# Weight splits on GpSimd instead of VectorE, and the low part of p ahead of the evacuations

## The chip, the cores and the metric

The kernel runs on one core of one Trainium2 chip. A core has a matrix engine (TensorE, "PE" in the profile, with its weight loads as "PEld"), a vector engine (VectorE, "DVE"), a scalar engine (ScalarE, "ACT"), a general engine (GpSimd, "POOL") and a queue engine (SyncE, "SP") that issues all DMA transfers of this kernel. Each engine takes its instructions strictly in the order in which the program lists them; engines wait for one another with semaphores. The metric is the device time of one execution in microseconds (us). The kernel before takes 931.03 us, the median of three runs from 930.53 to 931.16.

## The reference

```python
x  = A_x                                  # 1 x 2048 x 640, float32
xn = layernorm(x)
s  = attention(xn, wqkv, wo)              # 32 heads of 20, causal, window of 256 keys
h  = relu(xn @ w1 + b1) ** 2              # 640 -> 1536
g  = silu(h @ w2 + b2)                    # 1536 -> 640
return x + s * g
```

Here `attention` makes q, k and v with `xn @ wqkv`, takes a softmax over the keys that are at most 255 places behind a query, sums the values and multiplies with `wo`.

## The kernel before, in words

All products are made in pieces that together carry nearly float32 accuracy. A float32 operand is split into a high part (rounded to the matrix engine's float32 form) and a low part (the operand minus its high part); a product is then three matmuls, high by high, high by low and low by high. Splitting a weight therefore takes one ScalarE instruction that writes the high part and one subtraction that writes the low part. q, k and v are stored as three bfloat16 parts each and packed so that one matmul with 120 rows makes the scores of a head.

The program has three stretches. First (up to about 120 us) x is normalized and transposed, v is made for all rows, and q and k of the first group of heads. The weights of this stretch are split by `split_w` (line 177), whose subtraction is on GpSimd already. Then comes the main loop (lines 958 to 1009): 16 pairs of heads by 16 blocks of 128 rows give 256 steps and a dozen steps of run-out. A step works on five blocks of different age at once: the scores of block s (`scores`, L432) with their row maxima (`maxima`, L444, on VectorE); for the block of nine steps ago the transposed scores (`scores_t`, L476) and their exponentials p (`exps`, L483, on ScalarE) with the causal mask (L484 and L486, on GpSimd); for the block of ten steps ago the high half of p (`high`, L491, ScalarE); for that of eleven steps ago the low half (`low`, L497, VectorE, p minus its high half, called pl); and every second step the sums over the values (L511). The attention results are joined by three GpSimd instructions (L524, L525, L528) once in four steps and stored with a DMA (`o<-on`).

Attention alone does not fill TensorE, so each step also takes a portion of other matmuls from a generator, `filler`. Its stages, in order, are: q and k of the later groups of heads (`qkps`, L562), then for each half of the hidden layer and each quarter of the rows the first layer (`hps`, L562) and the second (`yps`, L824), and after the loop the output product (`wops`). `fill(amount)` hands out a fixed estimated time per step, so the order of the matmuls is fixed when the program is written, not while it runs. The results of a filler group leave PSUM in `evac` functions that are put on a list (`pending`, `late`) and emitted by `flush()` in the middle of the next step: for `qkps` a ScalarE copy and a VectorE subtraction (L730), later a GpSimd subtraction (L734, slo); for `hps` a ScalarE relu and square, a VectorE product (L782, sq) and a GpSimd subtraction (L783, hl); for `yps` a VectorE addition (L828).

The weights of the filler's stages are brought in pieces. `piece_pair` queues a piece that has its high and low part in one tile each (the q and k weights of a group and wo), `piece_lin` one whose parts lie in a row of tiles (w1 and w2, where a part can cross from one tile into the next and is then subtracted in two instructions). `issue` starts the DMA of a piece into one of three raw buffers; two steps later at the earliest `tick()` emits its split, at most one piece per step, in the middle of the step, ahead of the step's exponentials. In the loop there are two such pieces for each of three groups of heads, five for each half of w1, six for each half of w2 and five for wo: 33 pieces, 37 subtractions.

The middle of a step reads before the change:

```python
flush()
if d:
    low(*d)
tick()
if b:
    exs[b] = (exps(*b, *stp), stp[1])
```

Of the kernel before, what the change touches and what calls it, by code (L numbers as in the profile page):

```python
# [46 lines left out]
def f32(ap):  # L47
    return ap.bitcast(F32)
# [3 lines left out]
def attn_mlp_kernel(ctx: ExitStack, tc, x, wqkv, wo, w1, b1, w2, b2, out):  # L52
    nc = tc.nc
# [440 lines left out]
    def low(p, kb):  # L494
        ph, p32, n = phs.pop((p, kb))
        pl = at4.tile([P, 2, 3 * P], F16, tag="pl", bufs=PB - 1, name="pl")
        nc.vector.tensor_sub(pl[:, :, :n], p32[:, :, :n], ph[:, :, :n])  # L497
        pts[p, kb] = (ph, pl)
# [52 lines left out]
    def flush(upto=None):  # L551
        for f in late[:]:
            f()
        late.clear()
        while pending and (upto is None or flushed[0] < upto):
            flushed[0] += 1
            pending.pop(0)()
# [7 lines left out]
    def lin(tiles, off, n):  # L565
        done = 0
        while done < n:
            t, o = divmod(off + done, KC * BT)
            m = min(n - done, KC * BT - o)
            yield tiles[t][:, o:o + m], done, m  # L570
            done += m

    def lin1(tiles, off, n):
        t, o = divmod(off, KC * BT)
        return tiles[t][:, o:o + n]
# [5 lines left out]
    def issue(amount):  # L581
        credit[0] = min(credit[0] + amount, amount)
        while credit[0] > 0 and start_pieces(1):
            credit[0] -= 1.0
        while bulk and credit[0] > 0:
            cost, fn = bulk.pop(0)
            fn()
            credit[0] -= cost
# [27 lines left out]
    def release(n, force=False):  # L616
        done = []
        while started and len(done) < n:
            tag, at_, go = started[0]
            if not force and (tag in shut or state[2] < at_ + AGE):  # L620
                break
            done.append(started.pop(0)[2])
        return done

    def tick():
        for f in release(1):
            f()
            held[0] -= 1
# [9 lines left out]
    def piece(tag, src, go):  # L638
        def start():
            n = src.shape[-1]  # L640
            raw = wgt.tile([P, FHALF], F32, tag="wraw", bufs=RAW, name="raw")[:, :RAWN[tag[0]]]
            if len(src.shape) == 3:
                raw = raw.rearrange("p (c n) -> p c n", n=n)
            nc.sync.dma_start(raw, src)
            return lambda: go(raw)
        queue.append((tag, start))
# [3 lines left out]
    def piece_lin(tag, tiles, ohi, olo, src):  # L650
        n = src.shape[-1]

        def go(raw):
            t_ = tiles()
            for ap, o, m in lin(t_, ohi, n):
                nc.scalar.activation(ap, raw[:, o:o + m], AF.Copy)
            cuts = sorted({o for o in range(0, n + 1, P) if (ohi + o) % (KC * BT) == 0 or (olo + o) % (KC * BT) == 0} | {0, n})
            for c0, c1 in zip(cuts, cuts[1:]):
                nc.vector.tensor_sub(lin1(t_, olo + c0, c1 - c0), raw[:, c0:c1], f32(lin1(t_, ohi + c0, c1 - c0)))  # L659
        piece(tag, src, go)  # L660

    def piece_pair(tag, hi, lo, src):
        def go(raw):
            nc.scalar.activation(hi(), raw, AF.Copy)
            nc.vector.tensor_sub(lo(), raw, f32(hi()))
        piece(tag, src, go)

    def lazy(make):
# [282 lines left out]
    with tc.manual_schedule(engines={E_.PE, E_.Activation, E_.DVE, E_.Pool, E_.SP}):  # L951
# [6 lines left out]
        for s in range(steps):  # L958
# [32 lines left out]
                stp = scores_t(*b)  # L991
            post_all()
            issue(RATE)
            flush()
            if d:
                low(*d)
            tick()
            if b:
                exs[b] = (exps(*b, *stp), stp[1])
# [41 lines left out]
```

## Time and profile before

| | |
|---|---|
| time, median of 3 runs | 931.03 us (930.53 to 931.16) |
| the profiled execution: its time, its span | 931.16 us, 929.5 us |
| TensorE busy | 903.4 us, 97% |
| VectorE busy | 754.9 us, 81% |
| ScalarE busy | 670.0 us, 72% |
| GpSimd busy | 529.2 us, 57% |
| subtractions of weight pieces in the loop | 26 at L659, 11 at L665 |
| granted TensorE clock | 1.0 throughout |

The span runs from the first to the last instruction; 1.66 us of the execution lie outside it. An engine counts as busy while one of its instructions runs, also where that instruction has started and is held up; matmuls overlap, so a busy TensorE is not a TensorE at its peak, and waiting shows better in the time that a step takes than in the share. The chain of waits follows the end of the program back through what released each instruction. The tables by stretch give, for windows of the span, each engine's busy time and in brackets its number of instructions; asked for one line of the kernel, they give that line's alone. Since a step has two score matmuls at L432, their number tells the number of steps in a window.

### The profile page before, as it was taken

The numbers are of one execution on the slowest core, as the hardware profiler recorded it, in microseconds if no ns is written. First come the engines' busy times: TensorE is split into PE (matmuls) and PEld (weight loads), VectorE is DVE, ScalarE is ACT, GpSimd is POOL, SyncE is SP. The second block draws the span as 40 slices with busy tenths as digits, with TensorE's granted clock in tenths as the row PEclk, the third lists the DMA queues.
The fourth block names the chain that finished last, engine by engine and source line by source line (L and its number), as shares of the span: only waits on it lengthen the run. The fifth ranks groups of instructions, "written<-read, shape, count | busy, mean of one in ns | idle before, by whom it ended". The sixth has DMA issues, their size and how long they took to land.

```text
span 929.5 us, 21774 instructions
## 1 busy us (share of the span) xinstructions
PE 903.4 (97%) x7632; PEld 728.6 (78%) x7632; DVE 754.9 (81%) x2031; ACT 670.0 (72%) x1282; POOL 529.2 (57%) x832
## 2 busy tenths in 40 slices
PE   8999999999998899999999999999999999999998
PEld 7899976676665578788688778678688687789998
DVE  7695478989989988988888989987988988875554
ACT  5354338888988986987886987977987977984221
POOL 6010017887877884785774865885764965871000
PEclk9999999999999999999999999999999999999999
DMA  6998686677777454244254153365174264055873
GB/s 229 310 398 299 200 262 202 220 226 232 233 238 250 125 186 128 87 164 133 56 195 160 58 149 118 105 221 147 55 252 136 73 212 141 24 188 170 285 279 114
DMA packets 130803, 168.79 MB, mean 182 GB/s; under 512 B 44100, under 2 KB 91268, under 8 KB 128132
## 3 DMA queue, kind: packets, MB, share of 16 engines
q1 hardware_dynamic: 130692, 167.39, 55.1%
q8 instruction: 60, 0.98, 0.4%
q14 instruction: 51, 0.42, 0.1%
HBM read 96.15 MB, written 70.91 MB: 180 GB/s over the span
## 4 chain that ended last, share of the span: by engine, by line
PE 75%; DVE 12%; ACT 4%; DMA 3%; issue 3%; POOL 2%; SPq 1%; DVEq 0%; POOLq 0%; ACTq 0%
PE yps L824 15%; PE hps L562 13%; PE qkps L562 8%; PE wops L562 8%; PE sps L432 7%; PE ops L511 7%; PE stps L476 7%; PE vps L243 6%; DVE junk L444 3%; DVE pl L497 2%; DVE w L659 2%; PE qkps L201 1%; ACT p L483 1%; DVE st L142 1%; DMA xt<-in_A_x_dram 1%
## 5 line engine op out<-in xcount | busy, mean ns | idle before, releaser
L483 ACT ACTIVATE p<-stps,ebias 128x384 f32<-128x384 f32 (+2 forms) x512 | 258.4, 557 | 82.7 <-PE stps L476 69.9
L444 DVE CUSTOM_DVE_ANT_0 junk<-sps,mask 128x384 bf16<-128x384 f32 (+2 forms) x512 | 251.2, 527 | 62.7 <-PE sps L432 55.5
L497 DVE TENSOR_TENSOR pl<-p,ph 128x768 f16<-128x768 f32 (+2 forms) x256 | 241.0, 941 | 2.6 <-ACT ph L491 2.2
L484 POOL TENSOR_SCALAR_AFFINE_SELECT p<-p 128x256 f32<-128x256 f32 x256 | 145.9, 570 | 137.0 <-ACT p L483 127.6
L491 ACT ACTIVATE ph<-p 128x768 f16<-128x768 f32 (+2 forms) x256 | 206.0, 805 | 15.0 <-POOL p L486 13.2
L562 PE MATMUL hps<-xb,w 128*128 128x512 f32 x630 | 198.2, 430 | 0.0
L824 PE MATMUL yps<-w,hh 128*128 128x320 f32 x768 | 197.5, 330 | 0.0
L824 PEld LDWEIGHTS yps<-w,hh 128*128 128x128 f32 x768 | 132.1, 189 | 8.1 <-issue 1.5
L432 PE MATMUL sps<-ks,qs 120*128 120x384 bf16 (+2 forms) x512 | 127.5, 319 | 8.9 <-DVE mt L444 8.8
L562 PEld LDWEIGHTS hps<-xb,w 128*128 128x128 f32 x630 | 113.3, 189 | 21.2 <-issue 0.4
L476 PE MATMUL stps<-qs,ks 122*128 122x384 bf16 (+2 forms) x512 | 124.3, 322 | 3.2 <-ACT p L483 2.1
L824 PE MATMUL yps<-w,hl 128*128 128x320 f32 x384 | 126.6, 330 | 0.0
L783 POOL TENSOR_TENSOR hl<-sq,hh 128x256 fp32r<-128x256 f32 x96 | 104.2, 1086 | 39.0 <-DVE sq L782 26.3
L511 PEld LDWEIGHTS <-ph 128*128 128x128 f16 x1440 | 86.0, 97 | 26.4 <-issue 21.5
L486 POOL TENSOR_SCALAR_AFFINE_SELECT p<-p 128x256 f32<-128x256 f32 x224 | 105.3, 470 | 0.0
L511 PE MATMUL ops<-vp,ph 128*128 128x61 bf16 x1440 | 101.0, 192 | 0.0
L511 PE MATMUL ops<-vp,pl 128*128 128x61 bf16 x1440 | 99.7, 191 | 0.0
L511 PEld LDWEIGHTS <-pl 128*128 128x128 f16 x1440 | 87.8, 97 | 0.0
L824 PEld LDWEIGHTS yps<-w,hl 128*128 128x128 f32 x384 | 72.4, 189 | 4.9 <-issue 1.9
L476 PEld LDWEIGHTS <-ks 122*128 122x128 bf16 x512 | 30.1, 99 | 55.7 <-issue 45.8
L243 PE MATMUL vps<-wv,xT 128*128 128x320 f32 x480 | 72.1, 309 | 0.6 <-POOL wv L179 0.3
L243 PEld LDWEIGHTS vps<-wv,xT 128*128 128x128 f32 x480 | 70.5, 187 | 1.3 <-POOL wv L179 0.6
(116 smaller groups left out, 1491.6 us busy)
## 6 DMA issues: line engine op xcount, KB each, us to landing
ks<-k_d SPq DMA_DIRECT2D x64, 240.0 KB
qs<-q_d SPq DMA_DIRECT2D x64, 240.0 KB
xb<-xs SPq DMA_DIRECT2D x12, 1280.0 KB
xs<-xT SPq DMA_DIRECT2D x8, 1280.0 KB
y<-ysb SPq DMA_DIRECT2D x32, 320.0 KB
q_d<-shm SPq DMA_DIRECT2D x38, 256.0 KB
v_d<-vt SPq DMA_DIRECT2D x8, 976.0 KB
vp<-v_d SPq DMA_DIRECT2D x16, 488.0 KB
```

The costliest lines, as they stand in the source:

```text
L243: nc.tensor.matmul(ps, xT[xp][b][:, c * BT + t * P: c * BT + (t + 1) * P], wv[wp][:, c, nh * HALF:(nh + 1) * HALF], start=n == 1, stop=n = ...
L432: nc.tensor.matmul(ps[:, :nk], qs[i][0:KR, hh, q * P:(q + 1) * P], ks[i][0:KR, hh, k0 * P:k0 * P + nk], start=True, stop=True)
L444: nc.vector.tensor_tensor_reduce(out=junk[:, :nk], in0=r[hh][:, :nk], in1=mask[:, 3 * P - nk:], scale=1.0, scalar=-3.0e38, op0=ALU.add, op ...
L476: nc.tensor.matmul(ps[:, :n], ks[i][0:KR + 2, hh, kb * P:(kb + 1) * P], qs[i][0:KR + 2, hh, kb * P:kb * P + n], start=True, stop=True)
L483: nc.scalar.activation(p32[:, hh, :n], r[hh][:, :n], AF.Exp, scale=SCALE, bias=ebias)
L484: nc.gpsimd.affine_select(p32[:, :, 0:P], p32[:, :, 0:P], pattern=[[0, 2], [1, P]], compare_op=ALU.is_ge, fill=0.0, base=0, channel_multip ...
L486: nc.gpsimd.affine_select(p32[:, :, 2 * P:], p32[:, :, 2 * P:], pattern=[[0, 2], [-1, P]], compare_op=ALU.is_gt, fill=0.0, base=0, channel ...
L491: nc.scalar.activation(ph[:, :, :n], p32[:, :, :n], AF.Copy)
L497: nc.vector.tensor_sub(pl[:, :, :n], p32[:, :, :n], ph[:, :, :n])
L511: nc.tensor.matmul(ot[:, q % 4, hh, :], t[:, hh, (q - k) * P:(q - k + 1) * P], vp[:, k // 4, k % 4, hh, :], start=m == 1, stop=m == 2 * le ...
L562: nc.tensor.matmul(ps, a, b_, start=j == 0, stop=j == n - 1)
L824: nc.tensor.matmul(pss[nh], hs[fc][hp][:, tt * P:(tt + 1) * P], lin1(wt2, (wp * NFH + fc) * D + nh * HALF, HALF), start=fc == 0 and j == 0 ...
```

## The change

Two edits. The subtraction that makes the low part of a weight piece is issued on GpSimd instead of VectorE, in `piece_lin` and in `piece_pair`, at the same place of the program. And in every step `low` stands ahead of `flush()`, so that VectorE takes pl before the evacuations of that step.

```diff
@@ piece_lin
             for c0, c1 in zip(cuts, cuts[1:]):
-                nc.vector.tensor_sub(lin1(t_, olo + c0, c1 - c0), raw[:, c0:c1], f32(lin1(t_, ohi + c0, c1 - c0)))
+                nc.gpsimd.tensor_sub(lin1(t_, olo + c0, c1 - c0), raw[:, c0:c1], f32(lin1(t_, ohi + c0, c1 - c0)))
@@ piece_pair
             nc.scalar.activation(hi(), raw, AF.Copy)
-            nc.vector.tensor_sub(lo(), raw, f32(hi()))
+            nc.gpsimd.tensor_sub(lo(), raw, f32(hi()))
@@ main loop
             issue(RATE)
-            flush()
             if d:
                 low(*d)
+            flush()
             tick()
```

The instructions of TensorE and ScalarE stand in the same order as before. On GpSimd, in the stage that makes the first hidden half (`hps`) while w2 is brought in, one piece of the difference reads as follows (hl is the low part of the squared hidden values, w_0_2 a tile of w2's parts, p the exponentials under the mask):

```order
 L783 TENSOR_TENSOR hl<-sq,hh 128x256
+L659 TENSOR_TENSOR w_0_2_4658<-raw,w_0_0_4656 128x640
 L484 AFFINE_SELECT p_4773<-p_4773 128x2x128
 L486 AFFINE_SELECT p_4773<-p_4773 128x2x128
 L783 TENSOR_TENSOR hl<-sq,hh 128x256
+L659 TENSOR_TENSOR w_0_2_4658<-raw,w_0_0_4656 128x640
 L484 AFFINE_SELECT p_4835<-p_4835 128x2x128
 L486 AFFINE_SELECT p_4835<-p_4835 128x2x128
```

Each subtraction now stands on GpSimd ahead of the mask of the same step's exponentials and behind hl.

On VectorE the same place of the program, the step after, reads before (two maxima of scores, each with the read of its accumulator, open a step):

```order
L444 ISA junk,mt<-sps,mask 128x384
L444 ISA mt 128x1
L444 ISA junk,mt<-sps,mask 128x384
L444 ISA mt 128x1
L462 COPY mrow<-sps 16x128
L522 RECIPROCAL rs<-osb 128x8
L782 SCALAR_TENSOR_TENSOR sq<-hps,b1t,relu 128x256
L497 TENSOR_TENSOR pl<-p_4835,ph 128x768
L659 TENSOR_TENSOR w_0_2_4658<-raw,w_0_1_4657 128x640
```

and in the changed kernel:

```order
L444 ISA junk,mt<-sps,mask 128x384
L444 ISA mt 128x1
L444 ISA junk,mt<-sps,mask 128x384
L444 ISA mt 128x1
L462 COPY mrow<-sps 16x128
L522 RECIPROCAL rs<-osb 128x8
L497 TENSOR_TENSOR pl<-p_4835,ph 128x768
L782 SCALAR_TENSOR_TENSOR sq<-hps,b1t,relu 128x256
```

The subtraction is gone, and sq, which stood ahead of pl, stands behind it; the next step's maxima follow it directly.

## The prediction

> **What bounds the kernel now.** I read the page first, for the busy shares and the chain of waits.
>
> ```profile
> span 929.5 us, 21774 instructions
> PE 903.4 (97%) x7632; PEld 728.6 (78%) x7632; DVE 754.9 (81%) x2031; ACT 670.0 (72%) x1282; POOL 529.2 (57%) x832
> PE 75%; DVE 12%; ACT 4%; DMA 3%; issue 3%; POOL 2%; SPq 1%; DVEq 0%; POOLq 0%; ACTq 0%
> ```
>
> TensorE carries three quarters of the chain, so most steps go at its pace and nothing that happens on VectorE matters in them. The 12% of VectorE are the part that the change aims at. To see where they lie I listed the instructions at L659, which come in three stretches, and took the tables by stretch: first those three, then three undisturbed ones, one for each kind of filler (qkps, hps, yps). The columns are the stretch, its length, and busy time and number of instructions of PE, PEld, DVE, ACT and POOL.
>
> ```profile
> 273.20:322.30 49.10, 42.19 (x352) 28.21 (x352) 48.29 (x111) 43.77 (x81) 37.24 (x48) 1.00 0.62 195
> 539.70:559.20 19.50, 17.07 (x158) 14.28 (x156) 18.59 (x49) 17.04 (x31) 13.17 (x20) 1.00 0.53 159
> 575.50:595.40 19.90, 18.81 (x164) 13.00 (x164) 19.38 (x52) 19.03 (x39) 15.68 (x21) 1.00 0.39 121
> 225.40:273.20 47.80, 47.77 (x409) 33.36 (x408) 43.31 (x118) 40.32 (x75) 36.33 (x57) 1.00 0.75 233
> 376.50:403.20 26.70, 26.70 (x240) 18.74 (x236) 24.37 (x71) 25.89 (x54) 22.41 (x36) 1.00 0.23 66
> 483.80:502.60 18.80, 18.80 (x190) 16.61 (x186) 15.50 (x48) 12.21 (x24) 9.08 (x18) 1.00 0.42 133
> ```
>
> The same stretches, and two short ones with pieces of q and k weights, for the score matmuls at L432 alone (busy time of PE and PEld), of which a step has two:
>
> ```profile
> 273.20:322.30 49.10, 8.28 (x31) 2.74 (x32) 1.00 0.62 195
> 539.70:559.20 19.50, 3.29 (x13) 1.18 (x13) 1.00 0.53 159
> 575.50:595.40 19.90, 3.58 (x14) 1.15 (x15) 1.00 0.39 121
> 225.40:273.20 47.80, 8.81 (x36) 2.42 (x35) 1.00 0.75 233
> 376.50:403.20 26.70, 4.74 (x20) 1.31 (x20) 1.00 0.23 66
> 483.80:502.60 18.80, 3.54 (x14) 0.92 (x14) 1.00 0.42 133
> 175.60:182.10 6.50, 1.12 (x4) 0.38 (x5) 1.00 0.34 113
> 221.90:225.40 3.50, 0.66 (x2) 0.29 (x3) 1.00 0.33 112
> ```
>
> Undisturbed, a step takes 47.8/18 = 2.66, 26.7/10 = 2.67 and 18.8/7 = 2.69 us, whatever the filler: TensorE's pace. The first split stretch has 15 steps (an odd score matmul belongs to the next), so it would take 39.9 us and takes 49.1: 9.2 lost. The second has 6 steps, 16.1 against 19.5: 3.4 lost. The third has 7, 18.7 against 19.9: 1.2 lost. The two short ones lose 6.5 - 5.3 = 1.2 and 3.5 - 2.7 = 0.8. In all 15.8 us, the prize that is to be had. VectorE is busy for 48.29 of 49.1 us in the first stretch, and the chain runs through it there (start, length, instruction):
>
> ```profile
> 312.53 0.87 DVE pl L497
> 313.40 1.28 DVE w L659
> 314.68 0.47 DVE junk L444
> ```
>
> **The change part by part.** Removed from VectorE are 37 subtractions, added to GpSimd are the same 37. What one costs there the stage before the loop shows, with the same shape, and hl gives a second point (shortest, median and longest in ns):
>
> ```profile
> L179 POOL TENSOR_TENSOR wv<-wvr,wv x5: 1553/1578/1585, 13.5 to 20.0; 128x640 fp32r<-128x640 f32 x5
> L783 POOL TENSOR_TENSOR hl<-sq,hh x96: 727/1286/2054, 309.2 to 816.5; 128x256 fp32r<-128x256 f32 x96
> L659 DVE TENSOR_TENSOR w<-raw,w x26: 406/1025/1937, 276.6 to 593.6; 128x640 fp32r<-128x640 f32 x12, 128x768 fp32r<-128x768 f32 x6, 128x512 fp32r<-128x512 f32 x4, 128x256 fp32r<-128x256 f32 x4
> ```
>
> So 640 columns take 1.56 us. With (1553 - 727)/384 = 2.15 ns per column, 768 take about 1.83, 512 about 1.28 and 256 take 0.73; these are estimates from the two rows. A half of w1 (three whole pieces, two cut ones) is 3 x 1.83 + 2 x 2.01 = 9.5 us, a half of w2 6 x 1.56 = 9.4. The first stretch takes both, 18.9; the second a half of w1, 9.5; the third a half of w2, 9.4.
>
> VectorE then has room. What GpSimd needs besides I bound from both sides. Below: its mean per instruction in the undisturbed stretches, (36.33 + 22.41)/(57 + 36) = 0.632 us for qkps and hps, 9.08/18 = 0.504 for yps. Above: what its instructions took in the split stretches themselves, where VectorE held them up most. They do hold each other up:
>
> ```profile
> 499.28 0.95 DVE L497 TENSOR_TENSOR pl<-p,ph 128x768 f16<-128x768 f32 x1
> 499.55 0.95 POOL L484 TENSOR_SCALAR_AFFINE_SELECT p<-p 128x256 f32<-128x256 f32 x1 [1.97 <-ACT p L483]
> 500.45 0.40 POOL L486 TENSOR_SCALAR_AFFINE_SELECT p<-p 128x256 f32<-128x256 f32 x1
> ```
>
> The mask that starts inside pl ends 0.27 us behind it and takes 0.95 instead of 0.40. The subtractions on VectorE held GpSimd up in the same manner and no longer will, but a GpSimd that never rests meets every pl, so I take the middle. First stretch: 48 instructions, 30.3 to 37.2, middle 33.8, with the pieces 52.7 us. Second: 10.1 to 13.2, middle 11.6, with them 21.1. Third: 13.3 to 15.7, middle 14.5, with them 23.9. TensorE needs 39.9, 16.1 and 18.7: GpSimd becomes the longest in all three.
>
> How late GpSimd may be before TensorE waits, the undisturbed steps show. In hps:
>
> ```profile
> 516.91 0.40 POOL L486 TENSOR_SCALAR_AFFINE_SELECT p<-p 128x256 f32<-128x256 f32 x1
> 517.04 1.04 ACT L483 ACTIVATE p<-stps,ebias 128x384 f32<-128x384 f32 x2
> 517.97 0.84 ACT L491 ACTIVATE ph<-p 128x768 f16<-128x768 f32 x1
> 519.12 0.50 PE L476 MATMUL stps<-qs,ks 122*128 122x384 bf16 x2
> ```
>
> The mask ends at 517.31, its reader ph starts 0.66 later; exponentials end at 518.08, and the next transposed scores, which need their PSUM tiles, come 1.04 later. Behind ph ScalarE has no rest. Together 1.7 us. In yps:
>
> ```profile
> 502.98 0.40 POOL L486 TENSOR_SCALAR_AFFINE_SELECT p<-p 128x256 f32<-128x256 f32 x1
> 503.93 1.05 ACT L483 ACTIVATE p<-stps,ebias 128x384 f32<-128x384 f32 x2 [0.96 <-PE stps L476]
> 504.87 0.84 ACT L491 ACTIVATE ph<-p 128x768 f16<-128x768 f32 x1
> 505.94 0.50 PE L476 MATMUL stps<-qs,ks 122*128 122x384 bf16 x2
> ```
>
> 1.49 to ph, 0.96 of ScalarE's rest and 0.96 to TensorE make 3.4. Behind a late mask wait ph, all that ScalarE has queued behind it, and so the next steps' exponentials and TensorE; late hl and slo cost nothing by themselves.
>
> The stretches then take 52.7 - 1.7 = 51.0 (before 49.1, +1.9; from the ends -1.6 to +5.3), 21.1 - 3.4 = 17.7 (before 19.5, -1.8; -3.3 to -0.2) and 23.9 - 1.7 = 22.2 (before 19.9, +2.3; +1.1 to +3.5). Sum +2.4, from -3.8 to +8.6.
>
> The q and k pieces: two in successive steps put 3.1 us on GpSimd, which by 36.33/18 = 2.02 per step has 0.64 spare in each; the rest, 1.8, is about the tolerance. Of the 2.0 us lost there I take 1.5 as won (0 to 2.0).
>
> The wo pieces fall at the loop's end, where the chain runs through SP, whose queue holds raw loads behind the store of an attention result:
>
> ```profile
> 823.46 0.43 POOL on L528
> 823.91 0.38 SPq L542
> 824.38 3.13 DMA raw<-in_A_wo_dram
> 827.60 0.74 ACT L664 ACTIVATE wo4h<-raw 128x640 fp32r<-128x640 f32 x1 [0.96 <-DMA raw<-in_A_wo_dram]
> ```
>
> With two subtractions of 1.56 ahead of it that L528 comes up to 3.1 us later, less what VectorE's subtractions cost GpSimd before; between -1.0 (ScalarE's wait gone) and +2.0 I take +1.0.
>
> **pl ahead of the evacuations.** It needs only ph of the step before. Where ScalarE is late, pl filled its time behind sq; now it fills the wait for the relu:
>
> ```profile
> 334.99 0.48 DVE sq L782
> 335.48 0.86 DVE pl L497
> ```
>
> The chain has such a place at the end of three hps stages (near 335, 471 and 609 us), 0.48 each, so up to 1.4 is won. Against it sq, L730 and L828 come up to 0.95 later, and with sq hl, which GpSimd has queued ahead of its mask; but hl then no longer meets pl. I take -0.7.
>
> Sum: +2.4 - 1.5 + 1.0 - 0.7 = +1.2 on the profiled execution (931.16 us: span 929.5 and 1.66 around it; 0.13 above the median), so **932 us**; the bounds together give 923 to 943.
>
> [...]
>
> **The rivals.** (1) GpSimd's lateness reaches nobody. Then ScalarE and TensorE bound the stretches: 43.77 - 1.7 = 42.1 (ScalarE) for the first, 17.0 and 19.0 for the others, -7.0 - 2.5 - 0.9 = -10.4, with the other parts at their best (-2.0 - 1.4 - 1.0) -14.8: 916. For it speaks that VectorE is the engine in the chain; against it that GpSimd, 84% busy in undisturbed hps (22.41 of 26.7), gets half as much again. (2) Slower through SP: raw loads wait behind the store of an attention result, one in four steps. A piece is split two steps, 5.3 us, after its start and its load takes 3.13, so from 2.2 us of lateness at L528 on ScalarE stands still for a load, and everything behind it. Seven times in 28 steps, 0.96 each as at 827.60, +6.7: 939. (3) pl waits for whole subtractions, and VectorE gets nothing back: in the first stretch 48.29 less the 13 subtractions it loses, 13 x 1.03 = 13.3, plus 13 x 1.56 = 20.3 of waiting make 55.3, +6.2, half as much in the two others together: 940. Half the wait is likelier, and then GpSimd is the longer. That the change does not do what it says is out: the listing has the 37 instructions on the other queue.
>
> **How the numbers follow.** Forecast 0.55, rival (1) 0.18, (2) 0.20, (3) 0.07. The forecast's own range is 927 to 937; 0.2%, about 1.9 us, is what a measurement can tell from no change, and within the forecast 0.18 falls faster, 0.19 the same, 0.18 slower. With the rivals: faster 0.36, same 0.20, slower 0.44. The range reaches towards both rivals: 921 to 941.
>
> **What would show it.** Right: the first stretch within 47 to 53 us; POOL over 90% busy in it and VectorE under 85%; ph waiting for the masks (L486) in most split steps; TensorE's waits for L444 shrunk and those for the exponentials (L483) grown; the lost time at the q and k pieces gone. Wrong: a first stretch of 42 us with GpSimd late and nobody waiting (rival 1); ScalarE waiting for raw loads (2); pl of 2 us and more, VectorE still full (3).

## The result and the profile after

The changed kernel takes 946.79 us, the median of six runs (945.68 to 949.77); the kernel before, on the same chip, takes 930.89 (930.43 to 931.16). The ratio is 1.0173, with a 95% interval of 1.0161 to 1.0185: slower by 16 us. The forecast was 932 and the range ended at 941.

The page of the changed kernel answers to the one of before with these three lines (span, busy times, chain of waits by engine):

```profile
span 946.6 us, 21626 instructions
PE 911.1 (96%) x7632; PEld 732.2 (77%) x7632; DVE 753.6 (80%) x1994; ACT 670.2 (71%) x1282; POOL 559.3 (59%) x869
PE 65%; DVE 12%; ACT 9%; POOL 8%; issue 4%; DMA 2%; POOLq 0%; DVEq 0%; ACTq 0%
```

TensorE's part of the chain fell from 75% to 65%, ScalarE's rose from 4% to 9% and GpSimd's from 2% to 8%. VectorE lost 37 instructions and yet is as long busy as before (754.9): others of its instructions became longer.

The waits tell which way the loss goes. In the kernel before (waiting instruction, the one it waited for, us in total, how often, longest):

```profile
PE sps L432 <- DVE mt L444: 8.8, 20, 1.2
PE sps L458 <- DVE mp L449: 3.6, 7, 0.8
PE stps L476 <- ACT p L483: 2.1, 4, 0.7
ACT ph L491 <- POOL p L486: 13.2, 23, 1.2
DVE pl L497 <- ACT ph L491: 2.2, 4, 1.1
```

and in the changed kernel:

```profile
PE stps L476 <- ACT p L483: 13.6, 22, 2.7
PE sps L458 <- DVE mp L449: 7.0, 5, 2.7
PE sps L432 <- DVE mt L444: 1.7, 5, 0.7
ACT ph L491 <- POOL p L486: 39.8, 50, 2.6
DVE pl L497 <- ACT ph L491: 23.2, 29, 3.0
```

VectorE's row maxima (L444) hardly hold TensorE up any more (1.7 us instead of 8.8), as was wanted. In their place stands a row of waits: ph on GpSimd's mask, pl and the exponentials behind ph, TensorE behind the exponentials. TensorE also waits longer for L449, a short VectorE instruction that comes after the maxima of four blocks (7.0 us instead of 3.6).

The same 15 steps (60 to 74, where w1 and the first half of w2 are split), first of the kernel before, then of the changed one; the columns are stretch, length, busy time and number of instructions of PE, PEld, DVE, ACT, POOL, then the granted clock:

```profile
276.00:325.30 49.30, 42.23 (x336) 28.04 (x332) 48.98 (x113) 43.51 (x82) 39.26 (x51) 1.00 0.58 183
```

```profile
275.80:330.70 54.90, 45.95 (x335) 30.71 (x331) 41.43 (x98) 40.74 (x76) 49.45 (x59) 0.91 0.52 160
```

VectorE has become free (41 of 55 us), GpSimd is the fullest engine (49.5), but it too stands idle for 5.4 us. One place in the timeline of the changed kernel shows what happens (start, length, instruction, in brackets the idle time before it and what ended it):

```profile
280.00 1.89 POOL L734 TENSOR_TENSOR slo<-srt,shm 128x512 bf16<-128x512 f32 x1
...
281.85 1.98 POOL L659 TENSOR_TENSOR w<-raw,w 128x512 fp32r<-128x512 f32 x2
...
284.15 0.41 POOL L486 TENSOR_SCALAR_AFFINE_SELECT p<-p 128x256 f32<-128x256 f32 x1
...
284.58 0.84 ACT L491 ACTIVATE ph<-p 128x768 f16<-128x768 f32 x1 [2.59 <-POOL p L486]
284.94 1.81 POOL L659 TENSOR_TENSOR w<-raw,w 128x768 fp32r<-128x768 f32 x1
...
285.33 0.61 ACT L733 ACTIVATE shm<-srt 128x512 bf16<-128x512 f32 x1
...
285.46 2.10 DVE L497 TENSOR_TENSOR pl<-p,ph 128x768 f16<-128x768 f32 x1 [3.05 <-ACT ph L491]
285.85 0.92 ACT L656 ACTIVATE w<-raw 128x256 fp32r<-128x256 f32 x2
...
286.68 1.03 ACT L483 ACTIVATE p<-stps,ebias 128x384 f32<-128x384 f32 x2
...
287.29 0.32 PE L476 MATMUL stps<-qs,ks 122*128 122x384 bf16 x1 [2.74 <-ACT p L483]
```

slo and a piece's subtraction stand ahead of the mask; ph waits 2.59 us for it; behind ph ScalarE still has a copy of q (0.61) and the high part of the next piece (0.92) ahead of the exponentials; TensorE waits 2.74. pl, 0.95 us long in the undisturbed step at 499 us, starts here while the next subtraction runs and takes 2.10.

### The profile page after: what moved, and what is told of

Same layout as the page of the kernel before. It is cut to its first block, busy times and chain, and to the rows that moved or that the text cites. A ratio compares the mean times of both kernels' runs of the same rounds, so it can differ in the third digit from the quotient of the medians.

```text
span 946.6 us, 21626 instructions
## 1 busy us (share of the span) xinstructions
PE 911.1 (96%) x7632; PEld 732.2 (77%) x7632; DVE 753.6 (80%) x1994; ACT 670.2 (71%) x1282; POOL 559.3 (59%) x869
## 4 chain that ended last, share of the span: by engine, by line
PE 65%; DVE 12%; ACT 9%; POOL 8%; issue 4%; DMA 2%; POOLq 0%; DVEq 0%; ACTq 0%
PE yps L824 15%; PE hps L562 9%; PE wops L562 7%; PE qkps L562 7%; PE vps L243 6%; PE stps L476 6%; PE ops L511 6%; PE sps L432 6%; DVE pl L497 3%; ACT p L483 3%; DVE junk L444 3%; ACT ph L491 3%; POOL p L484 2%; POOL w L659 2%; PE qkps L201 1%
## 5 line engine op out<-in xcount | busy, mean ns | idle before, releaser
L483 ACT ACTIVATE p<-stps,ebias 128x384 f32<-128x384 f32 (+2 forms) x512 | 257.6, 555 | 70.1 <-PE stps L476 63.8
L444 DVE CUSTOM_DVE_ANT_0 junk<-sps,mask 128x384 bf16<-128x384 f32 (+2 forms) x512 | 250.8, 526 | 60.8 <-PE sps L432 54.3
L497 DVE TENSOR_TENSOR pl<-p,ph 128x768 f16<-128x768 f32 (+2 forms) x256 | 264.4, 1033 | 23.6 <-ACT ph L491 23.2
L491 ACT ACTIVATE ph<-p 128x768 f16<-128x768 f32 (+2 forms) x256 | 205.8, 804 | 48.2 <-POOL p L486 39.8
L484 POOL TENSOR_SCALAR_AFFINE_SELECT p<-p 128x256 f32<-128x256 f32 x256 | 153.8, 601 | 108.1 <-ACT p L483 99.7
L476 PE MATMUL stps<-qs,ks 122*128 122x384 bf16 (+2 forms) x512 | 128.7, 322 | 16.2 <-ACT p L483 13.6
L783 POOL TENSOR_TENSOR hl<-sq,hh 128x256 fp32r<-128x256 f32 x96 | 76.1, 794 | 50.9 <-DVE sq L782 30.1
L486 POOL TENSOR_SCALAR_AFFINE_SELECT p<-p 128x256 f32<-128x256 f32 x224 | 104.1, 465 | 0.0
```

The costliest lines, as they stand in the source:

```text
L444: nc.vector.tensor_tensor_reduce(out=junk[:, :nk], in0=r[hh][:, :nk], in1=mask[:, 3 * P - nk:], scale=1.0, scalar=-3.0e38, op0=ALU.add, op ...
L476: nc.tensor.matmul(ps[:, :n], ks[i][0:KR + 2, hh, kb * P:(kb + 1) * P], qs[i][0:KR + 2, hh, kb * P:kb * P + n], start=True, stop=True)
L483: nc.scalar.activation(p32[:, hh, :n], r[hh][:, :n], AF.Exp, scale=SCALE, bias=ebias)
L484: nc.gpsimd.affine_select(p32[:, :, 0:P], p32[:, :, 0:P], pattern=[[0, 2], [1, P]], compare_op=ALU.is_ge, fill=0.0, base=0, channel_multip ...
L486: nc.gpsimd.affine_select(p32[:, :, 2 * P:], p32[:, :, 2 * P:], pattern=[[0, 2], [-1, P]], compare_op=ALU.is_gt, fill=0.0, base=0, channel ...
L491: nc.scalar.activation(ph[:, :, :n], p32[:, :, :n], AF.Copy)
```

## The experiments

The runs were made on other chips, on which the kernel before takes 932.2 to 932.9 us (medians); every ratio below is against runs of it on the same chip. For the places of a loss I cut each trace into the loop's 256 steps at the score matmuls and took the differences to the trace of before, in us ("tail" is all behind step 254, "rest" the other steps behind 22, "ahead" what lies before the loop). Undisturbed steps agree to 0.01 us (221 of the 255 steps of e7 do), so sums of 0.3 mean something there; the column "ahead" is scatter.

| run | ratio | 0-22 | q, k pieces | 60-78 (I) | 155-166 (II) | 167-178 (III) | rest | tail | ahead |
|---|---|---|---|---|---|---|---|---|---|
| changed kernel | 1.0173 | +0.7 | -0.6 | +7.0 | +1.2 | +4.2 | +2.4 | +2.6 | -0.4 |
| e1 subtractions only | 1.0114 | 0.0 | -0.5 | +4.9 | +1.2 | +3.2 | +0.4 | +1.9 | +0.4 |
| e2 pl first only | 1.0016 | +0.7 | -0.6 | -0.9 | -0.7 | -0.1 | +2.9 | +0.6 | +1.1 |
| e3 mask first | 1.0196 | +0.7 | -0.8 | +5.3 | +3.2 | +3.3 | +1.9 | +4.4 | +0.3 |
| e5 chunks | 1.0307 | +1.1 | +1.1 | +9.4 | +3.2 | +6.1 | +2.4 | +5.3 | +1.8 |
| e6 alternate | 1.0035 | 0.0 | +0.4 | +0.1 | +0.7 | +2.2 | -0.3 | +0.4 | +0.6 |
| e7 pl first at splits | 0.9968 | +0.1 | -0.3 | -0.9 | -0.5 | -0.2 | -0.3 | -0.1 | +1.2 |
| e8 e6 and e7 | 1.0009 | 0.0 | +0.4 | -1.2 | +0.5 | +1.3 | +0.4 | -0.1 | +1.8 |
| e9 spread, VectorE | 0.9953 | +0.1 | 0.0 | -3.7 | -2.2 | -0.6 | +2.0 | +0.6 | +1.8 |
| e10 spread, GpSimd | 1.0133 | 0.0 | -0.5 | +3.7 | -0.2 | +2.3 | +3.4 | +2.8 | +1.0 |
| e11 e7 and e9 | 0.9925 | +0.1 | -0.3 | -4.4 | -1.9 | +0.1 | +0.8 | -0.3 | +0.4 |
| e12 one block less | 1.0112 | +0.1 | 0.0 | +4.1 | -0.6 | +2.3 | +3.4 | 0.0 | +1.6 |
| e13 e11, yps on GpSimd | 0.9946 | 0.0 | -0.3 | -5.1 | -0.5 | +0.1 | +0.7 | -0.3 | +1.9 |
| e14 lone pieces on GpSimd | 1.0048 | 0.0 | 0.0 | -2.0 | -0.6 | +2.4 | +5.0 | +0.9 | -0.3 |
| g3 halves | 1.0096 | -0.1 | -0.5 | +1.8 | -1.0 | +1.8 | +3.2 | +3.5 | +0.7 |

### Each edit alone

```diff
 e1: the subtractions as in the changed kernel, the order as before
-            if d:
-                low(*d)
             flush()
+            if d:
+                low(*d)
 e2: that order as in the changed kernel, the subtractions on nc.vector
```

> The first edit alone: the 37 subtractions on GpSimd, pl behind the evacuations as before. Theory A (the loss is GpSimd's: it is the longest engine where pieces are split, and its masks stand behind the subtractions): nearly all of the loss stays, 944 us, less only the small steps of loss outside the split stretches (sum of about 2.5 us in the trace of the changed kernel) which would belong to the second edit. Rival B (the second edit carries the loss, because sq, the L730 subtraction and hl come later behind pl and GpSimd's masks behind them): under 936 us.

> The second edit alone: pl ahead of the evacuations, the 37 subtractions on VectorE. Theory A: about no change, 930 to 932 us; if the small losses outside the split stretches (some 2.5 us in the changed kernel's trace) belong to this edit, 933.5. Rival B: most of the loss is here, over 940 us. The prediction had this edit at -0.7, so 930.2.

Measured: e1 943.0 us, ratio 1.0114 (1.0101 to 1.0128); e2 934.2, ratio 1.0016 (1.0007 to 1.0025). The first edit carries two thirds of the loss, and it makes the kernel slower by itself: rival B falls. But the second edit, which I had at -0.7 us, loses 1.5 alone, and the two together lose some 4 more than their sum (1.0173 against 1.0130). By the table e2 gains where pieces are split and loses elsewhere (0.7 and 2.9 us), and the extra loss of both lies in the split stretches: in I, +7.0 against 4.9 - 0.9, in III +4.2 against 3.2 - 0.1.

Where e2 loses, its timeline at the end of an hps stage shows (the last group is evacuated in two halves there, one behind the other):

```profile
747.58 0.48 DVE L782 SCALAR_TENSOR_TENSOR sq<-hps,b1t,relu 128x256 f32<-128x256 f32 x1 [0.30 <-ACT relu L779]
...
747.98 1.18 DVE L497 TENSOR_TENSOR pl<-p,ph 128x768 f16<-128x768 f32 x1
748.10 0.47 ACT L779 ACTIVATE relu<-hps,b1t 128x256 f32<-128x256 f32 x1 [0.17 <-DVE sq L782]
...
749.09 0.47 DVE L782 SCALAR_TENSOR_TENSOR sq<-hps,b1t,relu 128x256 f32<-128x256 f32 x1
749.44 1.45 POOL L783 TENSOR_TENSOR hl<-sq,hh 128x256 fp32r<-128x256 f32 x2
...
749.54 0.32 PE L476 MATMUL stps<-qs,ks 122*128 122x384 bf16 x1 [0.30 <-ACT p L483]
```

The second relu is done at 748.57, its sq starts at 749.09 because pl stands ahead, and hl, which GpSimd has queued ahead of its mask, at 749.44. The step takes 3.33 us instead of 2.75.

Why both together cost more follows from the same order: in the changed kernel hl waits for sq, sq for pl, pl for ph and ph for the mask, while the next mask waits on GpSimd behind hl. The order of before, with sq ahead of pl, has no such circle. One such place, first in the changed kernel, then the same hl in e1, where its sq runs from 312.99 to 313.47 and pl only behind it:

```profile
313.93 0.95 DVE L497 TENSOR_TENSOR pl<-p,ph 128x768 f16<-128x768 f32 x1
...
314.81 0.48 DVE L782 SCALAR_TENSOR_TENSOR sq<-hps,b1t,relu 128x256 f32<-128x256 f32 x1
...
315.42 0.74 POOL L783 TENSOR_TENSOR hl<-sq,hh 128x256 fp32r<-128x256 f32 x1 [2.08 <-ACT p L483]
```

```profile
313.61 1.32 POOL L783 TENSOR_TENSOR hl<-sq,hh 128x256 fp32r<-128x256 f32 x1 [0.30 <-ACT p L483]
```

(The profile names ScalarE as what ended the wait of 2.08; sq had ended 0.13 us ahead of hl.) GpSimd's idle time in steps 60 to 74 fits: 5.4 us in the changed kernel, 3.4 of it ahead of hl, and in e1

```profile
276.00:328.90 52.90, 44.59 (x335) 29.95 (x332) 41.69 (x98) 40.53 (x76) 50.57 (x59) 0.94 0.54 170
```

2.3, of which 0.3 ahead of hl. That it is this circle is argued from the order and these numbers; no run broke the circle alone.

### The order on GpSimd, and the length of a block

```diff
 e3: a step's subtraction behind its masks
-                nc.gpsimd.tensor_sub(...)
+                after.append(lambda ...: nc.gpsimd.tensor_sub(...))
...
                 exs[b] = (exps(*b, *stp), stp[1])
+            subtract()
 e5: four or five subtractions of 128 to 192 columns for one
+            cuts = sorted(set(cuts) | set(range(0, n, 160 if n == D else 192)))
             for c0, c1 in zip(cuts, cuts[1:]):
                 nc.gpsimd.tensor_sub(...)
```

> The changed kernel with one thing moved: the subtraction of a step stands behind that step's masks on GpSimd (the ScalarE copy of the piece stays where it was). The sum of GpSimd's work is the same. Theory A1 (the order counts: the mask waits in GpSimd's queue for a subtraction that nobody needs yet, then ScalarE's ph, the exponentials behind it, and TensorE): waits of ph for L486 fall back to some 15 us, the long TensorE waits and the half-clock windows vanish, time 934 us or less. Theory A2 (the sum counts: GpSimd is simply full in the stretches, so the masks are late behind whatever is in the queue): 944 us or more. [...]

> The changed kernel with every subtraction of a piece cut into four or five of 128 to 192 columns, so that none of them lasts longer than about 0.6 us. By the rows of L179 and L783 (0.18 us that does not go with the columns) this adds some 0.6 us of GpSimd time per piece, 20 us in all. Theory A (GpSimd's time decides): slower than the changed kernel, 950 us or more. Theory C (the length of a single hold decides: pl and the small VectorE operations at L448 and L449 wait until a whole subtraction is over): pl falls back to about 1.0 us, L449 to 0.2, and the time to 940 us or less.

Measured: e3 950.28 us, 1.0196 (1.0181 to 1.0212); e5 961.23, 1.0307 (1.0293 to 1.0321). A1 falls: it does not help to put the mask of the same step first, since the subtraction then stands ahead of the next step's. e3 also freed the raw buffers later, and ScalarE waited for raw loads, which the changed kernel does not:

```profile
ACT w L664 <- DMA raw<-in_B_w_dram: 6.5, 4, 2.7
```

so a part of its loss is not GpSimd's order. ph waited less often for masks than in the changed kernel (27.5 us instead of 39.8), and stretch I lost 5.3 instead of 7.0, far from what A1 wanted. Cutting the blocks short made it worse: GpSimd's busy time grew by 16 us (559.3 to 575.5) and the kernel's time by 12. Here TensorE's waits at L449 fell from 7.0 to 2.2 us, while those for the exponentials (L483) doubled, from 13.6 to 26.8. The length of a single hold does not decide.

### Half of the pieces, and another time for them

```diff
 e6: every second piece on GpSimd
-                nc.vector.tensor_sub(...)
+                eng.tensor_sub(...)      # nc.gpsimd for odd c and j and for k, else nc.vector
 e7: pl first only in a step with a split, subtractions on VectorE
+            if d and started_ready():
+                low(*d)
+                d = None
             flush()
             if d:
                 low(*d)
 e9: w1 and w2 in every second step at the most, on VectorE
     def tick():
+        if started and started[0][0][0] in "12" and state[2] < last_tick[0] + 2:
+            return
         for f in release(1):
+            last_tick[0] = state[2]
 e8: e6 with e7.  e10: e1 with e9.  e11: e7 with e9.
```

> The kernel before with every second subtraction of w1 and w2 on GpSimd, and of each pair of q and k weights the one for k; the other pieces, wo among them, and the order of pl stay as before. Theory A2 (a stretch lasts as long as its fullest engine works, plus a little): in steps 60 to 74 VectorE's 49.0 us fall by six subtractions to about 43, GpSimd's 39.3 rise to about 45, the stretch from 49.3 to about 46; the other stretches gain about 2 and 1, a k piece 0.5. Sum -5 to -7: ratio 0.993 to 0.995. Rival D (any subtraction on GpSimd makes a mask late and costs, however few there are): the stretches stay as long or get longer, ratio 1.000 to 1.006.

> The kernel before with pl ahead of the evacuations only in the steps in which a piece is split, all subtractions on VectorE. In the run with the second edit alone the steps with splits gained 2.3 us together (0.91 + 0.70 + 0.10 + 0.55) and the others lost 2.8 at the ends of stages. If the two are apart, the gain stays and the loss goes: -2 us, ratio about 0.998. If the gain was a shift by those losses: no change.

> The alternation of the subtractions and pl first in the steps with splits, together. If the two gains are apart they add: ratio 0.991 to 0.993. If pl first costs where GpSimd has subtractions, as it did in the changed kernel (+7.0 in steps 60 to 78 against +4.9 without it): no better than the alternation alone.

> The kernel before with the pieces of w1 and w2 split in every second step at the most, all subtractions on VectorE. Theory A2 in its other form (the stretches lose because the work of 11 pieces falls into 15 steps, on whichever engine): the pieces of w2 reach over more steps of the same stage, VectorE's work in steps 60 to 78 stays at 58 us and those 19 steps take 50.6 us undisturbed, so a gain of 1 to 2 us there and less elsewhere, ratio 0.997 to 0.999. If a piece costs its own time whenever it comes: no change.

> The subtractions on GpSimd, pl behind the evacuations as before, and the pieces of w1 and w2 split in every second step at the most. If what counts is GpSimd's work against the length of a stretch: 2.0 us of its other work and half of 1.6 per step are 2.8 against the 2.67 of a step, so the loss of the first edit (10.1 us) nearly goes, 931 to 935. If each subtraction costs by itself, because the mask behind it comes too late in that very step: 938 us or more, nearly what the first edit alone takes.

> All subtractions on VectorE; the pieces of w1 and w2 split in every second step at the most, and pl ahead of the evacuations in the steps with a split alone. Each of the two by itself gained (ratios 0.9953 and 0.9968). If they gain in different places they add up to about 0.993; if both only relieve VectorE in the same steps, no more than spreading alone, 0.995.

Measured: e6 1.0035 (1.0022 to 1.0047), e7 0.9968 (0.9955 to 0.9981), e8 1.0009 (1.0001 to 1.0018), e9 0.9953 (0.9939 to 0.9966), e10 1.0133 (1.0119 to 1.0147), e11 0.9925 (0.9911 to 0.9938).

e6 was the test of my picture of a fullest engine, and the picture fell: VectorE's work in steps 60 to 74 came down to 44.9 us and GpSimd's went up to 44.9 as expected, the stretch stayed at 49.1 instead of 46, and the kernel became slower. e9 shows the other side: the same 37 subtractions on VectorE, only further apart, bring the 15 steps down to 44.7 us, with VectorE as full as it can be (two of the eleven pieces then fall behind these steps; over steps 60 to 78, which hold all of them, the gain is 3.7):

```profile
277.90:322.60 44.70, 41.46 (x335) 27.84 (x331) 44.48 (x108) 41.49 (x79) 39.48 (x50) 1.00 0.67 204
```

On GpSimd (e10) the same spreading wins nothing. There the steps 64 to 69 take 26.3 us against 18.8 (the expectation of e12 below gives 27.1 for them), where three pieces meet in steps 66 to 68 at the change of stage; the steps 70 to 79, five pieces in every second step, 29.3 against 28.9. e7 keeps the gain of the second edit and loses its cost; e7 and e9 add up in e11, 925.18 us against 932.17, which beats both kernels. That changes no engine, only the time of the splits and of pl.

### The price of a block by itself

```diff
 g4, g5: the kernel before, with blocks of known length in single steps
             tick()
+            if s in PROBES:
+                for _ in range(PROBES[s]):
+                    nc.gpsimd.tensor_sub(probe, probe, probe)
 g3: e10, with each subtraction in two halves in successive steps
```

> The price by itself: the kernel before, with one, two, three or four subtractions of 256 columns on a scratch tile put on GpSimd ahead of the exponentials' masks in single steps far apart, in stretches where no weights are split (0.73 us each by the row of L783). Everything else is as before, the scratch output of the row maxima apart, which has one buffer instead of two for room. The prediction took GpSimd to be allowed 1.7 us of lateness in hps and 3.4 in yps. By that, one or two cost nothing anywhere, three (2.2 us) cost 0.5 us and four (2.9 us) 1.2 us in hps, and in yps all four are free. Theory P wants less room than that in hps: two (1.5 us) already cost 0.3 us or more.

> The same probes in other steps and with other numbers in them, mostly in steps of odd number, in which the sums over the values (24 of TensorE's instructions at L511) are made. Expected as in the other run of probes; with both a price can be read for each number of probes and each kind of filler.

> The spread subtractions on GpSimd once more, but each cut in two halves of 0.8 to 1.0 us that stand in two successive steps (the second one where the step would otherwise have none). GpSimd's work and the steps over which it reaches are those of the spread run (1.0133). Theory P (what costs is a whole subtraction of 1.5 to 2.0 us ahead of one mask, which with hl or slo ahead of it too makes the mask later than ph can bear): half of it stays within what ph can bear, so most of the loss goes, ratio 1.000 to 1.004. Theory S (GpSimd's sum counts): as the spread run, 1.012 to 1.015.

One to four probes lasted 0.6, 1.3, 2.0 to 2.8 and 3.0 to 3.5 us, a few of the ones and twos up to 1.5 and 2.0. What a probe cost is the sum over the step ahead of it, its own and the four behind:

| place | 1 | 2 | 3 | 4 |
|---|---|---|---|---|
| yps, behind its first two steps | 0.0 (6 times) | 0.0 (3), 0.1 | 0.0 (8), 0.3 | 0.0 (2) |
| hps, up to four steps before yps | 0.0 (2), 0.4 | 0.0 (3), 0.2 | - | 0.5 to 2.7 (10), mean 1.5 |
| the last three steps of hps, the first two of yps | 0.4, 0.8 | 0.0, 1.2, 1.6, 1.6 | 0.9, 1.3 | - |
| qkps | 0.3, 0.5 | 0.7 | 0.9, 2.7 | 0.3, 2.7 |

So the room that the prediction read from undisturbed steps, 3.4 us in yps and 1.7 in hps, is there: 2.6 us are free in yps, even 3.3 at its end (one block in a step in which the stage changes, one in the first step behind such a change), and in hps 3.3 cost 1.5. What the probes add is that at the end of an hps stage and in qkps there is hardly any room. (One pair of probes fell among the steps with splits and is left out; one loss of 1.1 us in qkps, in step 56, five steps behind four probes, lies outside the sums.) The two kernels took 961.65 and 956.07 us in one execution each. Of that, 9.4 and 10.7 us lie outside the sums, much of it in the same steps by the same amounts (1.2 in step 22, 1.35 in step 172): the price of the one thing that the two share besides probes, the single buffer for the scratch output of the maxima. How the delay travels, the place with four probes in hps shows:

```profile
397.40 3.41 POOL L1003 TENSOR_TENSOR probe<-probe 128x256 f32<-128x256 f32 x4
...
401.12 0.41 POOL L487 TENSOR_SCALAR_AFFINE_SELECT p<-p 128x256 f32<-128x256 f32 x1
...
401.56 0.84 ACT L492 ACTIVATE ph<-p 128x768 f16<-128x768 f32 x1 [3.45 <-POOL p L487]
...
403.12 1.03 ACT L484 ACTIVATE p<-stps,ebias 128x384 f32<-128x384 f32 x2
...
403.74 0.80 PE L477 MATMUL stps<-qs,ks 122*128 122x384 bf16 x2 [1.82 <-ACT p L484]
```

Mask, ph, exponentials, TensorE: the chain of the changed kernel, in a step of the order of before, with all splits on VectorE. g3 took 940.85 us, 1.0096 (1.0078 to 1.0115): halves are better than whole blocks (1.0133), but Theory P's 1.004 is missed too.

### ph without its wait

```diff
 f1: the changed kernel, f2: the kernel before, both with
-        nc.gpsimd.affine_select(p32[:, :, 0:P], p32[:, :, 0:P], ...)
+        pm = at2.tile([P, 2, P], F32, tag="pm", bufs=1, name="pm")
+        nc.gpsimd.affine_select(pm, p32[:, :, 0:P], ...)      # and the second mask likewise
```

> The changed kernel with the masks written to a scratch tile instead of p itself, so that GpSimd does the same work at the same places, but ScalarE's ph no longer waits for it. (p is then not masked: the kernel leaves that part of the computation out. The constant of the exponential is 0 so that the unmasked values stay finite, and the scratch output of the row maxima has one buffer instead of two for room.) Theory M (the loss goes through one wait: subtraction, mask behind it, ph behind the mask, the exponentials behind ph, TensorE): steps 60 to 78 fall from 66.8 to 58 us or less, and the time to 930 us or less, below the same edit of the kernel before. Rival T (GpSimd's lateness reaches TensorE by several ways: hl and slo, the store of an attention result, raw buffers that are freed late): the stretches stay long, 940 us or more.

> The same edit of the kernel before (masks to a scratch tile, ph free of them; the mask is left out of the computation). In steps 60 to 74 ph waits 1.5 us for masks there, so by Theory M it gains 1 to 4 us in all stretches together: 927 to 931 us. It is what the run before this one is to be compared with: by Theory M the changed kernel is then the faster of the two by 3 us or more, since VectorE has 37 subtractions less and nobody waits for GpSimd; by Rival T it is slower by 8 us or more.

Measured: f1 957.67 us, 1.0271 (1.0257 to 1.0285); f2 947.67, 1.0165 (1.0151 to 1.0179). Both leave the mask out of the computation. Both are slower than without the edit, so it did not do what it was meant to. Part of that is the single scratch buffer, which these two have as well: f2 loses 0.4, 0.5 and 1.35 us in steps 170 to 172, as do both probe kernels. The mask still reads p, and the exponentials that write the same buffer three steps later now wait for it; in f2

```profile
ACT p L483 <- POOL pm L487: 10.4, 14, 1.8
```

A wait of ScalarE for GpSimd was put in another place. f1 against f2 says little for the same reason: in steps 60 to 78 the two differ by 0.4 us, where the changed kernel and the one before differ by 7.0, but the whole still differs by 10. The question has to be answered by the other runs.

### Blocks that stand alone

```diff
 e12, e13, e14: e9 or e11 with the engine chosen for each piece
-                nc.vector.tensor_sub(...)
+                (nc.gpsimd if <choice> and not forced[0] else nc.vector).tensor_sub(...)
 e12: all of w1 and w2; e13: e11, second half of w1; e14: all but the first half of w1
```

> The spread subtractions of w1 and w2 on GpSimd, but the one piece that the change of stage forces (the last of w1, in step 67, between two others in steps 66 and 68) on VectorE; q, k and wo pieces on VectorE too. In the traces of the two spread runs the steps 64 to 69 take 27.1 us with the subtractions on GpSimd and 18.8 with them on VectorE, the steps 70 to 79 with five pieces in every second step 29.3 and 28.9. Theory L (lateness adds up: a block alone is free, blocks in successive steps are not): one block less among three takes about half of the 8.3 away, and wo gives 2 back, ratio about 1.006 to 1.009. Rival E (every piece on GpSimd costs about the same): one of 11 less, and wo, ratio 1.010 to 1.012.

> Spreading and pl first in the steps with splits (ratio 0.9925), with the five pieces of w1 that are split in the second yps stretch on GpSimd. The probes there cost nothing up to three (2.2 us). By Theory L, with two steps for each piece, the steps 155 to 166 stay within 0.5 us of the run without it, or gain: ratio 0.991 to 0.993. By Rival E, or by the trace of the spread run on GpSimd (1.4 us more than VectorE in steps 155 to 162), 0.994 to 0.995.

> The spread kernel (ratio 0.9953) with all pieces on GpSimd that stand alone, two steps from the next: w2 both times and the second half of w1; the first half of w1, whose pieces meet at the change of stage, stays on VectorE as do q, k and wo. Theory L: 17 pieces cost together 0 to 2 us, ratio 0.994 to 0.998. Rival E: 17 times the 0.3 us by which a piece of the first edit made the kernel slower (10.6 us over 33 pieces), ratio 1.001 or more.

Measured: e12 1.0112 (1.0099 to 1.0125), e13 0.9946 (0.9932 to 0.9959), e14 1.0048 (1.0035 to 1.0061). Rival E's numbers come out all three times, and Theory L falls. e14 puts on GpSimd only pieces that have two steps each, and is 8.7 us slower than e9 (936.90 against 928.24, on chips whose medians for the kernel before are equal): half a microsecond for each of 17 in the mean (7.3 us between the executions of both at a mean clock of 1.000). The single prices are far from even, so Rival E has the sum and not the picture: of the five pieces in yps two cost 1.0 each and one 0.6, and the five together 1.6, with what VectorE gains. The two appear in steps 158 and 160 (4.02 and 3.63 us, in e9 3.03 and 2.61). The first piece stands in the first whole step of yps, where three probes cost 0.9 too; the second stands two steps on, where probes of 2.6 us were free. So a piece is not a probe. Nor is it the meeting of three pieces alone: in e12, with the middle one back on VectorE, the steps 64 to 69 still take 26.6 us (e10 26.3, e9 18.8). The timeline of e14 around the first of the two:

```profile
543.86 1.84 POOL L667 TENSOR_TENSOR w<-raw,w 128x768 fp32r<-128x768 f32 x1
544.67 1.85 DVE L497 TENSOR_TENSOR pl<-p,ph 128x768 f16<-128x768 f32 x1
...
545.66 1.12 POOL L484 TENSOR_SCALAR_AFFINE_SELECT p<-p 128x256 f32<-128x256 f32 x1
...
547.17 0.84 ACT L491 ACTIVATE ph<-p 128x768 f16<-128x768 f32 x1 [1.72 <-POOL p L486]
...
547.92 0.83 ACT L664 ACTIVATE w<-raw 128x768 fp32r<-128x768 f32 x1
...
548.66 1.03 ACT L483 ACTIVATE p<-stps,ebias 128x384 f32<-128x384 f32 x2
549.27 0.79 PE L476 MATMUL stps<-qs,ks 122*128 122x384 bf16 x2 [0.84 <-ACT p L483]
```

and around the second, behind subtractions of 2.70 us:

```profile
553.51 0.84 ACT L491 ACTIVATE ph<-p 128x768 f16<-128x768 f32 x1 [2.02 <-POOL p L486]
...
554.26 0.83 ACT L664 ACTIVATE w<-raw 128x768 fp32r<-128x768 f32 x1
...
555.60 0.80 PE L476 MATMUL stps<-qs,ks 122*128 122x384 bf16 x2 [0.54 <-ACT p L483]
```

Two things are here that no probe's step had. ScalarE makes the high parts: both times 0.83 us of copy stand between ph and the exponentials, in a stage where ScalarE's rest is 0.96 per step. And around the first the engines hold each other up in turn: pl, started while the subtraction ran, took 1.85 us instead of 0.95, and the mask, started before pl ended at 546.52, took 1.12 instead of 0.40. What makes them do so no run shows. How the waits of 0.84 and 0.54 us divide between copy and holds is not settled: a probe next to a copy, and a piece whose high part another engine makes, were not tried.

## Why the prediction was wrong, point by point

**The prices** were right: a subtraction of 640 columns took 1.56 us in the mean of the 12 of w2, 1.53 to 1.58 for q and k (1.56 forecast), one of 768 columns 1.97 with its holds (1.83). **GpSimd's sum** lay within its bounds: 49.5 us in steps 60 to 74, where 49.2 to 56.1 had been forecast (52.7 in the middle). Most of the signs named at its end came: POOL at 90% there and VectorE at 75%, ph waiting for the masks (13.2 to 39.8 us), the waits for L444 nearly gone and those for L483 grown. Two did not: the stretch took 54.9 us and not 47 to 53, and of the 2.0 us lost at the q and k pieces only 0.5 went.

**The step that failed** is the sentence "The stretches then take 52.7 - 1.7 = 51.0", and its likes for 3.4 in yps. It took the room that undisturbed steps have and subtracted it from GpSimd's work in disturbed ones. The probes found the same room where it had been read. Where pieces are split it did not show. In the first stretch ph waited 9.1 us for masks (1.5 before), and ScalarE, whose queue holds the exponentials behind ph, had no rest in hps to make that up (25.89 of 26.70 us busy in the prediction's undisturbed stretch). By the lines of e14 the copy that belongs to every piece takes most of ScalarE's rest in yps, which was 0.96 of the 3.4 us, and holds are passed on (pl 1.85 us, the mask behind it 1.12); by the probes the end of hps and qkps have little room to begin with. Nor did GpSimd work without a rest, as the sum supposes: it stood idle itself, 1.7 us for slo and in the changed kernel 3.4 for hl (0.3 in e1). So instead of ending 1.7 us earlier than GpSimd's work, the first stretch ended 2.3 us (e1) or 5.4 us (changed kernel) later. By terms, forecast with bounds and measured, e1 first: stretch I +1.9 (-1.6 to +5.3), measured +4.9 and +7.0; II -1.8 (-3.3 to -0.2), +1.2 and +1.2; III +2.3 (+1.1 to +3.5), +3.2 and +4.2. (The measured steps reach a little further than the forecast's windows, since the delay does.) The second stretch has even the wrong sign. Together the three lost 12.4 of the 16 us, where +2.4 had been forecast. **q and k**: -1.5 forecast, -0.5 measured, within its bounds. **wo at the loop's end**: +1.0 (-1.0 to +2.0), measured +1.9 in e1 and 0.4 with wo on VectorE (e6).

**pl first**, -0.7, was wrong in sign: 1.5 us lost alone (e2). I had written down the cost, sq and hl later by up to 0.95, and priced it at less than the gain. The gain is real, but it lies in the steps with splits (e7), and the loss elsewhere, most of it at ends of hps stages (0.25 to 0.6 us at steps 80, 105, 130, 206 and 230). That the two edits together would cost 4 us beyond their sum was nowhere in the text: each was priced against the order of before.

**The rivals.** (1) is out, GpSimd's lateness reaches TensorE. (2), loads of pieces behind a store: no wait of ScalarE for a raw buffer in the changed kernel; it appeared in e3, where such waits came to 6.5 us for w1 and w2. (3), pl held by subtractions and VectorE getting nothing back: that each would hold pl for all of its 1.56 us was a supposition of mine; the holds are there (VectorE busy 753.6 us with 37 instructions less; pl 1.03 us in the mean, before 0.94), but VectorE had room for them in the first stretch, and short blocks did not help (e5). They did reach TensorE directly, through L449 (3.4 us more waiting there). The time that the rival gave, 940, was nearest, but through a full VectorE, which is not what happened.

What stays open: how much of a lone piece's price is the copy and how much the holds, and why some pieces cost 1.0 us and others nothing.

## What to carry to other kernels

Work moved to an engine that is on average idle has to be priced at the instruction that stands behind it in that engine's queue: who waits for that one, and what is queued behind the waiter. The room for lateness has to be read in the very steps that get the work, together with what else the move brings into them (here a copy on the waiter's own engine), since room found in quiet steps is spent by then. And where an engine is overfull for a few steps, moving the work in time can win (0.9953, with pl's order 0.9925) what moving it to another engine loses.

## What the runs showed of the hardware that was not expected

**TensorE's clock fell to one half around short waits.** The kernel before runs at 1.00 throughout its loop in its trace. In the changed kernel the granted clock drops to one half twice, behind the wait of 2.74 us that ended at 287.29 and during the one of 2.68 us that ended at 307.48 (columns as in the tables by stretch; the clock is the third number from the end):

```profile
308.00:313.00 5.00, 5.00 (x15) 3.15 (x14) 2.34 (x9) 3.20 (x7) 4.92 (x8) 0.52 0.59 170
```

The records of the clock put the slow spells at 288.95 to 292.37 and 306.02 to 312.85, 3.41 and 6.83 us long. The 3.41 us just ahead of each of them, and a third stretch of that length behind which no slow spell came:

```profile
285.54:288.95 3.41, 1.51 (x9) 0.92 (x9) 3.38 (x6) 2.91 (x6) 3.41 (x4) 1.00 0.83 190
302.61:306.02 3.41, 1.50 (x28) 0.80 (x26) 2.69 (x7) 2.65 (x6) 2.02 (x5) 1.00 1.04 333
609.81:613.22 3.41, 1.75 (x9) 1.08 (x7) 2.12 (x5) 2.97 (x6) 3.41 (x7) 1.00 0.44 95
```

TensorE was busy for 1.51 and 1.50 of 3.41 us in the first two, so idle for 56%, and for 1.75 in the third, idle for 49%. The longest of TensorE's waits at the two spells were those of 2.74 and 2.68 us. Why a slow spell came behind the first two stretches and none behind the third, the traces do not show. The forecast had no term for a lower clock.

What a slow spell cost was not the same everywhere. In the changed kernel and in e1 the times show no cost: the six executions of the changed kernel took 946.67 and 946.92 us at a mean clock of 0.998, 946.18 and 949.77 at 0.996, 945.68 at 0.995 and 948.28 at 0.993; those of e1 942.88 and 943.14 at 0.998 and 942.85 and 943.12 at 0.995. In e14 one did cost. From step 155 to 181 e12 and e14 are the same program and agree to 0.12 us in every step up to 179; then e14 has a slow spell, from 617.11 to 620.52, that e12 has not, and takes 1.5 us longer in steps 180 and 181 (e14 first):

```profile
613.27:622.73 9.46, 7.51 (x62) 6.24 (x59) 6.68 (x19) 7.56 (x15) 7.19 (x13) 0.82 0.82 261
```

```profile
621.37:629.28 7.91, 5.96 (x62) 4.88 (x59) 6.60 (x19) 7.23 (x14) 6.92 (x11) 1.00 0.91 284
```

So these 1.5 us of e14's trace are not the price of a piece. The executions of e13 go from 925.62 us at a mean clock of 1.000 to 929.62 at 0.996.

**A hold is passed on.** A VectorE instruction of eight columns at L449, 0.17 us in the median, took 1.46 us from 305.97 on, while a subtraction on GpSimd ran from 305.87 to 307.40, and TensorE waited 2.68 us for it (part of the 7.0 us at L458 above).
